# Cached attention and a Mish MLP with all gradients, one token: from a scheduled to a hand-ordered kernel

## The chip, the cores and the metric

The kernel runs on one core of a Trainium2 chip. The time is device microseconds of one execution; three executions of the kernel before took 449.38, 461.4 and 462.18 us, the median is 461.4 us. Lower is better. The profile is that of one execution.

## What is computed

One token `x` of width D = 640 goes through two branches that a gate mixes. Branch A has H = 32 heads of Dh = 128 over a cache of Sk = 4096 rows. All tensors are bf16.

```python
g = sigmoid((x * gate_w).sum(-1))
q = (x @ wq).reshape(32, 128)                    # per head
p = softmax(q @ K.T * Dh**-0.5)                  # 4096 scores of one query
a = (p @ V).reshape(4096) @ wo
h = x @ w1 + b1                                  # F = 1728
act = h * tanh(log1p(exp(-abs(h))) + max(h, 0))  # Mish
out = g * a + (1 - g) * (act @ w2)
```

The kernel returns `out` and, for a given `grad_out`, the gradients of x, K, V, wq, wo, w1, b1, w2 and gate_w. For the branch A and one head these are, with `do` the gradient of the head's output: `dp = V do`, `ds = p * (dp - sum(p * dp))`, `dq = K^T ds`, `dK = ds x q`, `dV = p x do` (outer products), `dwq = x x dq`, `dwo = o x da`. K and V are 33.5 MB each and are read once; dK and dV are as large and written once, so that the kernel moves some 168 MB.

## The kernel before

A cache row sits on partition p and block j: 128 partitions times J = 32 blocks of 128 elements. One head is one pass of `head` (L236), four heads are a group (G = 4), which shares one slice of wq and wo.

The instructions are written in a natural order and put into each engine's queue by the framework's scheduler, which goes by dependencies and priorities; the softmax statistics stand under `high_priority` (HP). It may place the next head's transposes among this head's work where buffers allow.

In a head, TensorE transposes K block by block (L254, 32 bf16 transposes of 128x128, eight to a PSUM tile; ScalarE copies a tile at a time, L255). Each transposed block is then the weight of a product with one moving column, q (L263, 32 of them), so that the scores lie as [128, 32]. The maximum over all rows needs the partitions: VectorE reduces along j (L268), ScalarE lays the result on a diagonal (L270, `dgm`), TensorE spreads it with a matrix of ones (L271, `MM`), VectorE takes the maximum (L273, `negM`). ScalarE's exponential (L275) gives e and its row sums, a product with ones their total (L276, `Zb`), then 1/Z (L278, `rz`) and p in duplicate (L280, `p_bf`). V goes the same way (L254, L255), its products with `do` (L285) give dp. L289 forms p*dp and its sums, L291 their total (`Db`), L293 and L295 ds. DQ (L298) and OP (L303) use K and V as they were loaded, 32 one-column products each, whose 32 result columns VectorE adds (L301, L306). Two small products per head take o to `a` (L311) and dq to dx (L315), the latter with transposed wq. The outer products (L324) are two halves of 2048 elements for dV and two for dK on VectorE, stored whole from GpSimd's queue (L332, L335). ScalarE forms the head's dwo (L336).

Per group, `prep_group` (L200) forms q on all partitions (L203, five 512-wide products), transposes wo (L193) to form `do` (L217), and transposes wq for dx; `finish_group` (L338) spreads dq by a diagonal from GpSimd (L340) and a product (L343), and VectorE forms dwq from PSUM (L347).

All K, V, wq and wo loads are on SyncE's queue, three heads ahead (four buffers for K and for V); a group's weights are asked for in the second head of the group before. The MLP's forward half runs after head 8 (L351), its gradients in six chunks, every third head from head 10 (L398), with the outer products for dw1 and dw2 on GpSimd (L419, L431); w1 is read once for the forward half and again in chunks (L353, L404).

## Time and profile before

| what | value |
|---|---|
| median of three executions | 461.4 us (449.38 to 462.18) |
| span of the profiled execution, first to last instruction | 459.0 us |
| time of the profiled execution as a whole | its span is what is recorded of it |
| mean granted clock of TensorE | 0.750 |
| TensorE, VectorE, ScalarE, GpSimd busy | 382.5, 264.4, 248.5, 96.3 us |
| DMA | 167.81 MB, mean 366 GB/s |
| L254, all transposes of K and V | 2048, 210.2 us |
| L324, all outer products | 128, 159.1 us |

A row of the groups reads: line, engine, operation, output and inputs, count, then busy time, mean ns of one, and how long the engine sat idle before it, and for whom. PEld is TensorE's weight load, which runs beside the matmul before it; a mean duration of a matmul holds its latency, so that neighbours overlap, and the *pitch*, the distance from one start to the next, is what a burst costs. Some pitches and durations that the timeline shows:

| operation | time |
|---|---|
| bf16 transpose, 128 columns, clock 1.0 / 0.5 | pitch 55 / 107 ns |
| one-column product, bf16 | pitch 25 / 27 ns |
| 512-wide product | pitch 216 / 427 ns |
| fp32 weight load (L271), clock 1.0 / 0.5 | 108 / 217 ns |
| fp32 product 128 wide (L271), two passes | 327 ns |
| outer half (L324) | 1.25 us, pitch 1.14 |
| copy 128x512 (L255) | 583 ns, pitch 482 |
| 128x512 product from PSUM (L347) | 682 ns, pitch 598 |
| 96x640 sum (L415) | 870 ns, pitch 800 |
| dwo of a head (L336) | 828 ns, pitch 730 |
| table load of ScalarE, five of them | 1283 ns each |
| DMA packet of 8192 / 5120 / 1280 / 1024 B | 309 / 199 / 55 / 46 ns |

### The profile page before, as it was taken

The page shows a single profiled execution, that of the slowest core. Times are in us where ns is not written, and L with a number is a line of the kernel's source. Part 1 is how long each engine was busy: PE and PEld are TensorE (multiplying, and loading weights), DVE is VectorE, ACT ScalarE, POOL GpSimd, SP SyncE. Part 2 cuts the span into 40 slices and gives each one's busy share as a digit, 9 for nine tenths or more (in the row PEclk, how much of TensorE's full clock was granted, in tenths as well). Part 3 has the DMA queues.
Part 4 walks back from the last instruction along what each step waited for, and adds up shares of the span by engine and source line. Part 5 has one row for each costly group of instructions (what it writes and reads, how often), then busy time and mean ns, then how long its engine had stood idle before and what let it go on. Part 6 is the DMA issues. An engine that isn't in the chain of part 4 may idle for free.

```text
span 459.0 us, 16426 instructions
## 1 busy us (share of the span) xinstructions
PE 382.5 (83%) x7301; PEld 350.4 (76%) x7320; DVE 264.4 (58%) x693; ACT 248.5 (54%) x571; POOL 96.3 (21%) x109
## 2 busy tenths in 40 slices
PE   0898989959899899969989599899999959999930
PEld 0688969838798788858888588887999858989820
DVE  0355735633627357737477488565656736665782
ACT  1575766626717777534665356656756536654510
POOL 0001010100100443551317141041000501014020
PEclk9998988859956699665987579587955879655555
DMA  8979999999999999999999999999999999973593
GB/s 248 427 308 349 411 425 417 413 416 334 418 422 360 369 360 363 420 354 406 420 418 370 386 386 375 420 406 394 413 424 419 364 348 347 416 284 127 206 365 118
DMA packets 45560, 167.81 MB, mean 366 GB/s; under 512 B 3122, under 2 KB 27506, under 8 KB 29106
## 3 DMA queue, kind: packets, MB, share of 16 engines
q1 hardware_dynamic: 25161, 84.24, 48.5%
q0 software_dynamic: 10368, 71.54, 38.0%
q10 hardware_dynamic: 9961, 10.99, 7.0%
q8 instruction: 57, 0.93, 0.8%
q14 instruction: 13, 0.11, 0.1%
HBM read 84.73 MB, written 82.03 MB: 363 GB/s over the span
## 4 chain that ended last, share of the span: by engine, by line
PE 61%; DMA 22%; ACT 7%; DVE 6%; issue 3%; ACTq 0%; SPq 0%; DVEq 0%
PE tr L254 25%; DMA wq_g<-in_A_wq_dram 10%; PE wtr_ps L193 6%; DMA wo_g<-in_A_wo_dram 5%; PE ss L298 5%; PE ss L285 5%; PE ss L303 5%; PE ss L263 4%; DMA w2c<-in_B_w_dram 3%; PE qbc_ps L203 3%; PE dobc_ps L217 2%; DMA xg_bc<-in_gate_w_dram 2%; PE ss L271 2%; ACT VT L255 2%; ACT KT L255 2%
## 5 line engine op out<-in xcount | busy, mean ns | idle before, releaser
L254 PE MATMUL tr<-ident_bf,Kn 128*128 128x128 bf16 x1024 | 105.1, 250 | 3.8 <-issue 1.2
L254 PE MATMUL tr<-ident_bf,Vn 128*128 128x128 bf16 x1024 | 105.1, 256 | 3.9 <-ACT VT L255 3.2
L255 ACT COPY VT<-tr 128x512 f32<-128x512 f32 x128 | 74.0, 583 | 53.0 <-PE tr L254 51.4
L255 ACT COPY KT<-tr 128x512 f32<-128x512 f32 x128 | 73.5, 585 | 42.3 <-PE tr L254 41.4
L254 PEld LDWEIGHTS <-Kn 128*128 128x128 bf16 x1024 | 81.0, 116 | 7.9 <-issue 6.1
L254 PEld LDWEIGHTS <-Vn 128*128 128x128 bf16 x1024 | 80.6, 117 | 5.9 <-issue 4.2
L324 DVE TENSOR_TENSOR dV_sb<-p_bf,qd_sb 128x2048 bf16<-128x2048 bf16 x64 | 80.6, 1264 | 4.8 <-ACT p_bf L280 4.8
L324 DVE TENSOR_TENSOR dK_sb<-ds_bf,qd_sb 128x2048 bf16<-128x2048 bf16 x64 | 78.5, 1229 | 0.3
L332 POOL DMA_DIRECT2D out_dram<-dV_sb x32 | 17.8, 555 | 164.4 <-DVE negD L293 80.4
L335 POOL DMA_DIRECT2D out_dram<-dK_sb x32 | 17.4, 544 | 144.5 <-DVE dK_sb L324 76.8
L263 PE MATMUL ss<-qTs_g,KT 128*128 128x1 bf16 x1024 | 40.9, 165 | 3.9 <-issue 2.1
L263 PEld LDWEIGHTS <-KT 128*128 128x128 bf16 x1024 | 37.3, 101 | 5.2 <-issue 3.0
L285 PEld LDWEIGHTS <-VT 128*128 128x128 bf16 x1024 | 34.1, 100 | 4.5 <-issue 2.3
L285 PE MATMUL ss<-doTs_g,VT 128*128 128x1 bf16 x1024 | 34.5, 164 | 2.1 <-ACT VT L255 1.1
L298 PEld LDWEIGHTS <-Kn 128*128 128x128 bf16 x1024 | 30.7, 99 | 6.6 <-issue 5.7
L298 PE MATMUL ss<-ds_bf,Kn 128*128 128x1 bf16 x1024 | 31.5, 164 | 4.6 <-issue 2.6
L303 PEld LDWEIGHTS <-Vn 128*128 128x128 bf16 x1024 | 31.2, 100 | 1.8 <-issue 1.4
L303 PE MATMUL ss<-e_bf,Vn 128*128 128x1 bf16 x1024 | 31.8, 164 | 0.7 <-issue 0.4
L347 DVE TENSOR_TENSOR dwq_g<-dqbc_ps,cols_f 128x512 bf16<-128x512 f32 x40 | 26.1, 682 | 5.6 <-DMA out_dram<-dwq_g 4.2
L203 PE MATMUL qbc_ps<-wq_g,cols_bf 128*128 128x512 bf16 x33 | 14.0, 535 | 16.2 <-DMA wq_g<-in_A_wq_dram 8.3
L273 DVE TENSOR_REDUCE negM<-ss 128x1 f32<-128x128 f32 x32 | 9.3, 290 | 30.9 <-PE ss L271 30.9
L278 DVE RECIPROCAL rz<-ss 128x1 f32<-128x1 f32 x32 | 5.4, 169 | 30.8 <-PE ss L276 30.8
(331 smaller groups left out, 522.2 us busy)
## 6 DMA issues: line engine op xcount, KB each, us to landing
Kn<-in_A_k_cache_dram SPq DMA_DIRECT2D x32, 1024.0 KB, 9.5
Vn<-in_A_v_cache_dram SPq DMA_DIRECT2D x32, 1024.0 KB, 16.1
out_dram<-dV_sb POOLq DMA_DIRECT2D x32, 1024.0 KB, 9.7
out_dram<-dK_sb POOLq DMA_DIRECT2D x32, 1024.0 KB, 10.2
wq_g<-in_A_wq_dram SPq DMA_DIRECT2D x8, 640.0 KB
wo_g<-in_A_wo_dram SPq DMA_DIRECT2D x8, 640.0 KB, 16.5
out_dram<-dwo_g ACTq DMA_DIRECT2D x8, 640.0 KB, 11.6
out_dram<-dwq_g ACTq DMA_DIRECT2D x8, 640.0 KB, 3.3
```

Source lines behind the costliest of these rows:

```text
L193: nc.tensor.transpose(tp[:, t, :], blocks[i + t], ident_bf[:])
L203: nc.tensor.matmul(qbc_ps[:], lhsT=x_col_bf[:, rc:rc + 1].to_broadcast([P, P]), rhs=wq_g[:, rc, :], start=(rc == 0), stop=(rc == RC - 1))
L254: nc.tensor.transpose(tp[:, t, :], src[:, c * TB + t, :], ident_bf[:])
L255: nc.scalar.copy(f32view(dst[:, c * TB:(c + 1) * TB, :].rearrange("p a b -> p (a b)")), f32view(tp[:].rearrange("p a b -> p (a b)")),)
L263: nc.tensor.matmul(S[:, j:j + 1], lhsT=KT[:, j, :], rhs=gp["qTs_g"][:, hh:hh + 1], start=True, stop=True)
L285: nc.tensor.matmul(DP[:, j:j + 1], lhsT=VT[:, j, :], rhs=gp["doTs_g"][:, hh:hh + 1], start=True, stop=True)
L298: nc.tensor.matmul(DQ[:, j:j + 1], lhsT=Kn[:, j, :], rhs=ds_bf[:, j, 0:1], start=True, stop=True)
L303: nc.tensor.matmul(OP[:, j:j + 1], lhsT=Vn[:, j, :], rhs=e_t[:, j:j + 1], start=True, stop=True)
L324: nc.vector.tensor_tensor(dst[:, a:b, :].rearrange("p j (a b) -> p j a b", b=2), colsrc[:, a:b, :].unsqueeze(2).to_broadcast([P, n, Dh // ...
L332: nc.gpsimd.dma_start(dVv[h], dV_sb[:])
L335: nc.gpsimd.dma_start(dKv[h], dK_sb[:])
L347: nc.vector.tensor_tensor(dwq_g[:, rc, :], dqbc_ps[:], x_col_f[:, rc:rc + 1].to_broadcast([P, GD]), ALU.mult)
```

## The change

The function is written anew. `manual_schedule()` puts the instructions into each engine's queue in the order of the program. The parts:

- **Pair transposes.** K and V are viewed as fp32, two bf16 values to an element, and transposed in 16 fp32 transposes of 128x128 instead of 32 of bf16, through three PSUM buffers. The copies stay 128x512 of fp32, four to an operand. Even and odd elements then lie interleaved, so a product takes every second bf16 as its weights, two products accumulate a pair of blocks, and q and do are laid out in zero-padded pairs of columns (`qd`, `dd`).
- **64-wide products.** All products of a head have a moving operand of 64 columns, one or two columns repeated. DQ and OP accumulate over the 32 blocks in PSUM, so that one column is the result and no reduction follows.
- **wq and wo untransposed.** Rows of wo are regrouped so that do comes from four 640-wide sums on VectorE per group (`prep_do_stt`), dx from five 512-wide sums (`fin_dx`); dwq comes from a copied row in SBUF (`fin_dwq`). `a` is formed once per group (`fin_orow`).
- **Order.** `period(h)` is a head without its K part. The next head's K transposes and products are in it: a quarter of the transposes before `Db`, a quarter after OP, the rest with all products after DQ. Group and MLP work is in three slots: A after `negM`, B after DQ, C after dK.
- **Queues.** wq and wo are loaded from ScalarE's queue, dwq and dwo stored from GpSimd's; V has three buffers, K four; V(h+3) and K(h+4) are asked for at the end of head h.
- **MLP.** w1 is read once and whole, w2 in two halves; all outer products and sums are on VectorE, spread over heads 5 to 30, with the 1728-wide dx sums in heads 27 and 29. Mish is formed from exponentials alone, without the logarithm, tanh and sigmoid.

```diff
+wq_v = A_wq.rearrange("(p rc) c -> p rc c", p=P)
...
+wo_v = A_wo.rearrange("(g p i) n -> g p i n", p=P, i=G)
...
+ctx.enter_context(tc.manual_schedule())
...
+def load_wq(g, eng):
+    wqs[g] = wts.tile([P, RC, GD], BF16, name="wq_g", tag="wq_g")
+    eng.dma_start(wqs[g][:], wq_v[:, :, g * GD:(g + 1) * GD])
+def load_wo(g, eng):
+    wos[g] = wts.tile([P, G, D], BF16, name="wo_g", tag="wo_g")
+    eng.dma_start(wos[g][:], wo_v[g])
...
-            nc.tensor.transpose(tp[:, t, :], blocks[i + t], ident_bf[:])
...
-        nc.tensor.transpose(qT_ps[:, hh, 0:1], qd_sb[0:1, 0, hh * Dh:(hh + 1) * Dh], ident_bf[0:1, 0:1])
...
-        nc.tensor.matmul(dobc_ps[:], lhsT=da_col_bf[:, c:c + 1].to_broadcast([P, P]),
-                         rhs=woT_g[:, c, :], start=(c == 0), stop=(c == RC - 1))
...
+    for rc in range(RC):
+        nc.tensor.matmul(ps[:], lhsT=x_col[:, rc:rc + 1].to_broadcast([P, P]), rhs=wqs[g][:, rc, :],
+                         start=(rc == 0), stop=(rc == RC - 1))
+    row = wts.tile([P, GD + Dh], BF16, name="qrow", tag="qrow")
+    nc.scalar.copy(row[:, 0:GD], ps[:])
+    nc.scalar.copy(row[0:1, GD:GD + Dh], ps[0:1, 0:Dh])
...
+    for hh in range(G):
+        nc.tensor.transpose(cp[:, hh:hh + 1], rf[0:1, hh * 64:hh * 64 + P], ident_f[0:1, 0:1])
...
+    nc.scalar.mul(dst[0:64, :, :, 0], cpb[0:64], mul)
...
+    nc.vector.scalar_tensor_tensor(junk[:], in0=wos[g][:, i, :], scalar=1.0, in1=da_bc[:], op0=ALU.mult,
+                                   op1=ALU.mult, accum_out=dof[g][:, i:i + 1])
...
+    for i in range(G):
+        nc.tensor.matmul(ps[:, i * P:(i + 1) * P], lhsT=dob[:, i:i + 1].to_broadcast([P, P]), rhs=ident[:],
+                         start=True, stop=True)
...
+    nc.scalar.copy(row[:, 0:GD].rearrange("m (p i) -> m p i", i=G), pv)
+    nc.scalar.copy(row[0:1, GD:GD + Dh].rearrange("m (p i) -> m p i", i=G), pv[0:1, 0:Dh // G, :])
...
+    for hh in range(G):
+        nc.tensor.matmul(ps[:, hh * P:(hh + 1) * P], lhsT=obfs[g][:, hh:hh + 1].to_broadcast([P, P]), rhs=ident[:],
+                         start=True, stop=True)
+    orow = small.tile([1, GD], BF16, name="orow", tag="orow")
+    nc.scalar.copy(orow[:], ps[0:1, :])
...
+    for i in range(G):
+        nc.tensor.transpose(op[:, i, 0:1], ov[:, i, :], ident[0:1, 0:1])
...
+    nc.vector.tensor_copy(opb[:], op[:, :, 0])
+    opf = small.tile([P, G], F32, name="opf", tag="opf")
+    nc.vector.tensor_copy(opf[:], opb[:])
...
+    for c in range(RC):
+        for i in range(G):
+            nc.tensor.matmul(ap[:, c:c + 1], lhsT=wos[g][:, i, c * P:(c + 1) * P], rhs=opb[:, i:i + 1],
+                             start=(i == 0), stop=(i == G - 1))
+    nc.vector.tensor_tensor(aT_acc[:], aT_acc[:], ap[:], ALU.add)
...
+    nc.scalar.activation(dwos[g][:, i, :], da_bc[:], ACT.Copy, scale=osc[g][:, i:i + 1])
...
+    for hh in range(G):
+        nc.tensor.matmul(ps[:, hh * P:(hh + 1) * P], lhsT=dqbfs[g][:, hh:hh + 1].to_broadcast([P, P]), rhs=ident[:],
+                         start=True, stop=True)
+    row = wts1.tile([P, GD], BF16, name="dqrow", tag="dqrow")
+    nc.scalar.copy(row[:], ps[:])
...
+    nc.vector.tensor_scalar(dwqs[g][:, rc, :], dqrow[g][:], x_col_f[:, rc:rc + 1], None, ALU.mult)
...
+    nc.vector.scalar_tensor_tensor(junk[:, 0:GD], in0=wqs[g][:, rc, :], scalar=1.0, in1=dqrow[g][:], op0=ALU.mult,
+                                   op1=ALU.mult, accum_out=dx_parts[:, rc, g:g + 1])
...
-                nc.tensor.transpose(tp[:, t, :], src[:, c * TB + t, :], ident_bf[:])
-            nc.scalar.copy(
-                f32view(dst[:, c * TB:(c + 1) * TB, :].rearrange("p a b -> p (a b)")),
-                f32view(tp[:].rearrange("p a b -> p (a b)")),
-            )
...
-        nc.tensor.matmul(S[:, j:j + 1], lhsT=KT[:, j, :], rhs=gp["qTs_g"][:, hh:hh + 1], start=True, stop=True)
...
-        nc.tensor.matmul(DQ[:, j:j + 1], lhsT=Kn[:, j, :], rhs=ds_bf[:, j, 0:1], start=True, stop=True)
...
-            nc.vector.reduce_sum(st["dq_bf_g"][:, hh:hh + 1], DQ, axis=AX.X)
...
-    nc.vector.tensor_scalar(ojunk[:], OP, rz[:], None, ALU.mult, ALU.add, accum_out=o32[:])
...
-        nc.tensor.matmul(aTp[:, c:c + 1], lhsT=gp["wo_g"][:, hh, c * P:(c + 1) * P], rhs=o_bf[:, 0:1],
-                         start=True, stop=True)
...
-        nc.tensor.matmul(dxTp[:, rc:rc + 1], lhsT=gp["wqT_g"][:, hh, rc, :], rhs=st["dq_bf_g"][:, hh:hh + 1],
-                         start=True, stop=True)
...
-    nc.gpsimd.tensor_tensor(diag[:], ident_bf[:].unsqueeze(1).to_broadcast([P, G, P]),
-                            st["dq_bf_g"][:].unsqueeze(2).to_broadcast([P, G, P]), ALU.mult)
...
-        nc.vector.tensor_tensor(dwq_g[:, rc, :], dqbc_ps[:], x_col_f[:, rc:rc + 1].to_broadcast([P, GD]), ALU.mult)
...
+def transposes(src, dst, c):
+    tp = tr_ps.tile([P, 4, P], F32, name="tr", tag="tr")
+    sf = f32v(src[:].rearrange("p j d -> p (j d)"))
+    for t in range(4):
+        jp = 4 * c + t
+        nc.tensor.transpose(tp[:, t, :], sf[:, jp * P:(jp + 1) * P], ident_f[:])
+    nc.scalar.copy(dst[:, 4 * c:4 * c + 4, :], tp[:])
+def products(T_, cols, dst, c):
+    tb = T_[:].bitcast(BF16).rearrange("r a (p b) -> r a p b", b=2)
+    for t in range(4):
+        jp = 4 * c + t
+        for par in range(2):
+            nc.tensor.matmul(dst[:, 2 * jp:2 * jp + W], lhsT=tb[:, jp, :, par],
+                             rhs=cols[:, par, :].unsqueeze(1).to_broadcast([P, W // 2, 2]),
+                             start=(par == 0), stop=(par == 1))
...
+    nc.vector.reduce_max(m32[:], S, axis=AX.X)
+    dgm = small.tile([P, P], F32, name="dgm", tag="dgm", bufs=2)
+    nc.scalar.activation(dgm[:], ident_s[:], ACT.Copy, scale=m32[:])
+    transposes(Vn, VT, 0)
+    transposes(Vn, VT, 1)
+    nc.tensor.matmul(MM, lhsT=ones_f[:], rhs=dgm[:], start=True, stop=True)
+    negM = small1("negM")
+    nc.vector.tensor_reduce(negM[:], MM, axis=AX.X, op=ALU.max, negate=True)
+    run(h, "A")
+    e_bf = small.tile([P, J], BF16, name="e_bf", tag="e_bf")
+    rowsum = small1("rowsum")
+    nc.scalar.activation(e_bf[:], S, ACT.Exp, bias=negM[:], scale=scale, accum_out=rowsum[:])
+    transposes(Vn, VT, 2)
+    transposes(Vn, VT, 3)
+    ddc = dds[g % 2][:, hh]
+    products(VT, ddc, sv[:, 0:128], 0)
+    products(VT, ddc, sv[:, 0:128], 1)
+    nc.tensor.matmul(Zb, lhsT=ones_f[:], rhs=rowsum[:], start=True, stop=True)
+    rz = small1("rz")
+    nc.vector.reciprocal(rz[:], Zb)
+    p_bf = small.tile([P, J, 2], BF16, name="p_bf", tag="p_bf")
+    nc.scalar.activation(p_bf[:], e_bf[:].unsqueeze(2).to_broadcast([P, J, 2]), ACT.Copy, scale=rz[:])
+    products(VT, ddc, sv[:, 0:128], 2)
+    products(VT, ddc, sv[:, 0:128], 3)
+    dV = outs.tile([P, J, Dh], BF16, name="dV", tag="dV")
+    dorow = dorows[g][:, hh * Dh:(hh + 1) * Dh]
+    outer(dV, p_bf, dorow, 0, HJ)
...
+    nc.vector.scalar_tensor_tensor(pj[:], in0=DP, scalar=1.0, in1=e_bf[:], op0=ALU.mult, op1=ALU.mult,
+                                   accum_out=part[:])
+    outer(dV, p_bf, dorow, HJ, J)
+    nc.gpsimd.dma_start(dVv[h], dV[:])
+    if h + 1 < H:
+        k_transposes(h + 1, 0)
+    nc.tensor.matmul(Db, lhsT=ones_f[:], rhs=part[:], start=True, stop=True)
+    for j in range(J):
+        nc.tensor.matmul(OP, lhsT=Vn[:, j, :], rhs=e_bf[:, j:j + 1].to_broadcast([P, W]),
+                         start=(j == 0), stop=(j == J - 1))
+    if h + 1 < H:
+        k_transposes(h + 1, 1)
+    negD = small1("negD")
+    nc.vector.tensor_scalar(negD[:], Db, rz[:], -1.0, ALU.mult, ALU.mult)
+    ds_bf = small.tile([P, J, 2], BF16, name="ds_bf", tag="ds_bf")
+    nc.vector.scalar_tensor_tensor(ds_bf[:], in0=DP.unsqueeze(2).to_broadcast([P, J, 2]), scalar=negD[:],
+                                   in1=p_bf[:], op0=ALU.add, op1=ALU.mult)
+    for j in range(J):
+        nc.tensor.matmul(DQ, lhsT=Kn[:, j, :], rhs=ds_bf[:, j, 0:1].to_broadcast([P, W]),
+                         start=(j == 0), stop=(j == J - 1))
+    run(h, "B")
+    if h + 1 < H:
+        for c in range(4):
+            if c < 2:
+                k_transposes(h + 1, c + 2)
+            k_products(h + 1, c)
+    dK = outs.tile([P, J, Dh], BF16, name="dK", tag="dK")
+    qrow = qrows[g][:, hh * Dh:(hh + 1) * Dh]
+    outer(dK, ds_bf, qrow, 0, HJ)
+    nc.vector.tensor_copy(dqbfs[g][:, hh:hh + 1], DQ[:, 0:1])
+    nc.vector.tensor_scalar(obfs[g][:, hh:hh + 1], OP[:, 0:1], rz[:], None, ALU.mult)
+    outer(dK, ds_bf, qrow, HJ, J)
+    nc.gpsimd.dma_start(dKv[h], dK[:])
+    run(h, "C")
+for g in range(NG - 1):
+    h0 = G * g
+    if g >= 1:
+        at(h0 + 1, "A", load_wo, g + 1, nc.scalar)
+        at(h0 + 1, "C", load_wq, g + 1, nc.scalar)
+    for i in range(2):
+        at(h0 + 2, "C", prep_do_stt, g + 1, i)
+        at(h0 + 3, "A", prep_do_stt, g + 1, 2 + i)
+    at(h0 + 3, "A", prep_q, g + 1)
+    at(h0 + 3, "B", prep_qcols, g + 1)
+    at(h0 + 3, "C", prep_do_row, g + 1)
+    at(h0 + 3, "C", prep_docols, g + 1)
+    f0 = h0 + G
+    at(f0, "A", fin_orow, g)
+    at(f0, "B", fin_dqrow, g)
+    for i in range(G):
+        at(f0, "C", fin_dwo, g, i)
+    at(f0, "C", store_dwo, g, nc.gpsimd)
+    for rc in range(RC):
+        at(f0, "C", fin_dwq, g, rc)
+    at(f0, "C", store_dwq, g, nc.gpsimd)
+    for rc in range(2):
+        at(f0, "C", fin_dx, g, rc)
+    for rc in range(2, RC):
+        at(f0 + 1, "A", fin_dx, g, rc)
...
-    nc.sync.dma_start(w1_sb[:], w1_v)
...
-    nc.sync.dma_start(w2c[:], w2_v[:, f0:f1, :])
-    w1c = mlp.tile([P, RC, FW], BF16, name="w1c", tag="w1c")
-    nc.sync.dma_start(w1c[:], w1_v[:, :, c * FW:(c + 1) * FW])
...
-        nc.vector.scalar_tensor_tensor(junk[:], in0=w2c[:, i, :], scalar=dm[:, f0 + i:f0 + i + 1], in1=dbp[:],
-                                       op0=ALU.mult, op1=ALU.mult, accum_out=ms["dh32"][:, f0 + i:f0 + i + 1])
...
-    nc.gpsimd.tensor_tensor(dw2c[:], act_bf[:, f0:f1].unsqueeze(2).to_broadcast([FP, FCC, D]),
-                            db_bc_bf[0:FP, :].unsqueeze(1).to_broadcast([FP, FCC, D]), ALU.mult)
-    nc.gpsimd.dma_start(dw2_v[:, f0:f1, :], dw2c[:])
...
-    nc.gpsimd.tensor_tensor(dw1c[:], dh_bc[:].unsqueeze(1).to_broadcast([P, RC, FW]),
-                            x_col_f.unsqueeze(2).to_broadcast([P, RC, FW]), ALU.mult)
-    nc.gpsimd.dma_start(dw1_v[:, :, c * FW:(c + 1) * FW], dw1c[:])
...
-        nc.vector.scalar_tensor_tensor(junk2[:], in0=w1c[:, rc, :], scalar=1.0,
-                                       in1=dhbc_ps[:], op0=ALU.mult, op1=ALU.mult,
...
+    nc.sync.dma_start(ml["w1"][:], w1_v)
...
+        nc.tensor.matmul(ps[0:n, 0:1], lhsT=lw, rhs=x_col[:, rc:rc + 1], start=(rc == 0), stop=(rc == RC - 1))
...
+    nc.vector.scalar_tensor_tensor(junk[0:n, :], in0=w, scalar=ml["dm"][0:n, i:i + 1], in1=db_bc[0:n, :],
+                                   op0=ALU.mult, op1=ALU.mult, accum_out=ml["dhf"][0:n, i:i + 1])
...
+            nc.tensor.matmul(ps[:, c:c + 1], lhsT=w[:, c * P:(c + 1) * P], rhs=ml["act"][0:n, i:i + 1],
...
+    nc.vector.tensor_scalar(w, db_bc[0:n, :], ml["actf"][0:n, i:i + 1], None, ALU.mult)
...
+    nc.vector.scalar_tensor_tensor(w, in0=w, scalar=1.0, in1=ml["dhrow"][:], op0=ALU.mult, op1=ALU.mult,
+                                   accum_out=dx_parts[:, rc, NG:NG + 1])
...
+    nc.vector.tensor_scalar(ml["w1"][:, rc, :], ml["dhrow"][:], x_col_f[:, rc:rc + 1], None, ALU.mult)
...
+M0 = 5
+for i in range(NF):
+    at(M0 + i // 5, "B", mlp_h, i)
+at(M0 + 4, "C", mlp_act)
+mp = [h for h in range(M0 + 5, 31) if h % 4 in (1, 2, 3)]
...
+    for i in (2 * k, 2 * k + 1):
+        if i < FH:
+            at(mp[k], "C", mlp_dh, i)
...
+for rc in range(RC):
+    at(mp[13] if rc < 3 else mp[14], "C", mlp_dx, rc)
+    at(mp[13] if rc < 3 else mp[14], "C", mlp_dw1, rc)
...
+prep_q(0)
+prep_qcols(0)
+for i in range(G):
+    prep_do_stt(0, i)
+prep_do_row(0)
+prep_docols(0)
+for c in range(4):
+    k_transposes(0, c)
+for c in range(4):
+    k_products(0, c)
+load_wq(1, nc.scalar)
+load_wo(1, nc.scalar)
+for h in range(H):
+    period(h)
+    if h + 3 < H:
+        load_v(h + 3)
+    if h + 4 < H:
+        load_k(h + 4)
+    if h == 1:
+        mlp_load_w1()
+    if h == 4:
+        mlp_load_w2(0)
...
+g = NG - 1
+mlp_store_dw1(nc.sync)
+mlp_store_dw2(1, nc.sync)
+fin_orow(g)
+for i in range(G):
+    fin_dwo(g, i)
+store_dwo(g, nc.sync)
+fin_dqrow(g)
+for rc in range(RC):
+    fin_dwq(g, rc)
+store_dwq(g, nc.sync)
+for rc in range(RC):
+    fin_dx(g, rc)
```

## The prediction

> **What bounds the kernel now.** I read three views in this order: the page's busy table with its chain, the groups, and the windows with their granted clock.
>
> ```profile
> PE 382.5 (83%) x7301; PEld 350.4 (76%) x7320; DVE 264.4 (58%) x693; ACT 248.5 (54%) x571; POOL 96.3 (21%) x109
> ...
> PEclk9998988859956699665987579587955879655555
> ...
> DMA packets 45560, 167.81 MB, mean 366 GB/s; under 512 B 3122, under 2 KB 27506, under 8 KB 29106
> ...
> PE 61%; DMA 22%; ACT 7%; DVE 6%; issue 3%; ACTq 0%; SPq 0%; DVEq 0%
> ```
>
> TensorE is busy for 83% of the span and holds 61% of the chain; the transfers hold 22%, mostly in the wait for the next group's wq and wo. Two limits lie close together. The queues' packets fill 94.4% of 16 engines' span (the shares of section 3 added), about 433 us, and TensorE fills 383 us. The PEclk row is the third thing to see: 9s at the start, only 5s in the last five slices.
>
> ```profile
> L254 PE MATMUL tr<-ident_bf,Kn 128*128 128x128 bf16 x1024 | 105.1, 250 | 3.8 <-issue 1.2
> L254 PE MATMUL tr<-ident_bf,Vn 128*128 128x128 bf16 x1024 | 105.1, 256 | 3.9 <-ACT VT L255 3.2
> L255 ACT COPY VT<-tr 128x512 f32<-128x512 f32 x128 | 74.0, 583 | 53.0 <-PE tr L254 51.4
> ...
> L324 DVE TENSOR_TENSOR dV_sb<-p_bf,qd_sb 128x2048 bf16<-128x2048 bf16 x64 | 80.6, 1264 | 4.8 <-ACT p_bf L280 4.8
> ...
> L347 DVE TENSOR_TENSOR dwq_g<-dqbc_ps,cols_f 128x512 bf16<-128x512 f32 x40 | 26.1, 682 | 5.6 <-DMA out_dram<-dwq_g 4.2
> ```
>
> 2048 transposes take 210 us of TensorE; this is what the change halves in number. The outer products on VectorE stay as they are.
>
> The windows show the granted clock (columns: window, its length, then busy us of PE, PEld, DVE, ACT and POOL, then clock, DMA share, GB/s):
>
> ```profile
> 58.00:61.40 3.40, 3.35 (x65) 2.61 (x63) 2.90 (x7) 2.77 (x6) 0.53 (x1) 1.00 1.01 426
> ...
> 93.10:96.50 3.40, 0.00 (x0) 0.00 (x0) 1.12 (x1) 0.00 (x0) 0.53 (x1) 0.52 1.04 421
> 391.70:404.00 12.30, 12.30 (x261) 12.22 (x261) 7.00 (x19) 7.51 (x17) 1.06 (x2) 0.58 1.01 416
> ```
>
> The clock is 1.0 or 0.5 in stretches of 3.41 us. In the third window TensorE is busy without a gap and yet has 0.58, so busy time does not earn the clock. Counting the moving columns of the matmul records in each stretch does separate the cases: full-clock stretches with at most 2626 columns were followed by half clock, those with at least 2852 stayed, so about 835 columns per us are needed. One-column products (32 take 0.94 us) stream almost nothing. A head of before streams 64 transposes x 128 = 8192 columns, 128 of its products, 256 of the maximum matmul and some 2690 of group work, 11,270 in 14.3 us (459/32), or 790 per us: just under the line, which is the mean clock of 0.75.
>
> The Trainium skill, "TensorE: Matmul & The Clock Gate", Part 1, has the clock fall after an idle window of about 3.4 us; by it the third window above would have kept full speed and so would nearly all of the new kernel, which by it comes to the 445 worked out below, by the columns to 474. The measured 0.58 decides against that.
>
> **The chain of a plain head.** The new kernel runs in written order, so I laid one head out by before's rows, with 0.04 us from engine to engine (read from the timeline). reduce_max 0.19, dgm 0.40, then ACT holds the copies of two V blocks ahead of the exponential (0.58 and 0.48), exponential 0.38, two more copies 1.06, p 0.35: 3.6 us with the steps between. MM, negM, Zb and rz (0.33, 0.29, 0.24, 0.17) lie beside the copies. Then VectorE does half of dV 1.25, pj 0.19, the other half 1.14, negD 0.16, ds 0.28: 6.6. From there TensorE needs DQ (32 at 25 to 27 ns, 0.85), eight transposes of the next K and 32 products 0.85, against dK on VectorE (1.25, 1.14 and two small ones), which ends at 9.2.
>
> **The pair transpose** is not in the trace. The bounds: a bf16 128-column transpose has a pitch of 55 ns at full clock, the lower end; an fp32 weight load (L271) takes 108 ns, its pair of passes 327 ns. I take 108 ns, since a pair transpose has to load 128x128 of fp32 as L271 does, and keep 55 and 213 (two such loads) for the range. Eight then cost 0.86 on the chain, and the head ends at **9.4 us**; with 55 ns 8.8. Sixteen per operand instead of 32 thus cost the same 1.7 us by 108 ns: the halving is worth nothing on TensorE unless the pitch is the lower one.
>
> The same page, "Weight-path perf modes", says the fast weight load is off for FP32; this speaks against the pair form. By its rule the load is the slow one, as L271's row has it; the sum with it is the one above, without it 10 us lower over the kernel.
>
> The **64-wide products** cost 26.7 ns at full clock against 25 for one column (the weight load bounds both), 53 against 27 at half clock. They bring columns: 32 transposes x 128, 128 products x 64 and 256 make 12,540 per head. If a plain head runs 9.4 us that is 1330 per us, well over 835. The weights of the K and V products are read with a step of two elements; no row has that. At best nothing is lost, at worst they load like fp32 (108 ns): 64 x 83 = 5.3 us per head. I take nothing, since every bf16 row of 128 columns shows the 25 ns pitch, and keep a loss for the range. The column reductions L301 and L306 become small copies, under 0.2 us a head gained.
>
> **Group work.** It leaves 40 transposes, five 512-wide dobc matmuls and L194's copies per group on TensorE and ACT, and comes back on VectorE in the chain. Per group, by the rows: the o row before the exponential makes VectorE and TensorE wait for each other (four matmuls, a copy, four transposes, two copies, 20 products: 1.9 us); dwq (five SBUF-only scalar products; between L278's 169 ns for one column and the 444 ns of a 128x288 sum, L436; taken 0.25) and two dx sums (0.6, L347's pitch) 2.5, and the dq row 0.3; three more dx sums 1.8; four 640-wide do sums (0.8 each, L415's pitch) and q's row 2.9. That is 9.4 per group, 66 for seven.
>
> **The MLP** was on POOL, PE and DVE beside the heads; now it is in the chain: h 14 x 0.5, the activation as some 24 dependent small operations 4.5, dh 14 x 0.8, dw2 14 x 0.3, b 1.8, the dh row 3.0, five 1728-wide dx sums 1.9 each (1728 elements at the rate of L415's 640 in 0.67 above its start) and five dw1 0.55: 43 us. The four table loads of 1.28 us saved count for nothing more than 5.
>
> **The sum at full clock.** Head 0's maximum came at 24.6 us; now wo lands at about 9, then four sums 3.3, row and columns 1.5, K's transposes and products 3.4: 17. 31 heads x 9.4 = 291. Side work 66 + 43 - 5 = 104. After the last maximum: the head 9.4, o row 1.9, dq row 0.9, dwq and dx 4.3, small operations 2.5, transposes and copies 1.2, the store 2: 22. Together 434.
>
> Transfers: K, V, dK and dV in 8192-byte packets of 309 ns are 2048 packets over 16 engines, 9.9 us a head, 316 us; the weights and the rest at their rows' medians some 82: 398, and 420 with the 5% by which before's queues exceed this. w1 is loaded once, not twice. The floor is below 434, but loads are issued at a head's end behind others, and w1's 2.2 MB stand ahead of K. The three plain heads in a row near the start outrun the queue. I add 11 of 0 to 16: **445**.
>
> **The clock.** In a long head VectorE's last slot lies between dK and the next maximum; V's first eight transposes run ahead into three PSUM buffers and then TensorE waits for the maximum: 1.1 us of dK, 2.5 of side work and 0.6, over 4 us without columns in a finishing head, more beside dx of the MLP (13 us of it at head 27). The following stretch is then at half clock. There a head needs 32 x 0.216 + 128 x 0.053 + 1.5 = 15.2 us of TensorE, so a stretch of 3.41 us yields 3.41 x 9.4/15.7 = 2.05 and loses 1.36. Some 17 heads last over 12 us; with 1.3 such stretches after each, 22 x 1.36 = 30. The sum is **474 us** against the span of 459.0, which lies 2.4 below the median of 461.4; I leave this within the range.
>
> **Rivals.** *The clock stays up* (chance 0.27, the one on the other side): the 64-wide columns fill enough of each stretch, or a pair transpose counts more than 128 columns. For it: 12,540 columns a head. Against it: VectorE's slots leave over 4 us empty. It gives 434 to 452. It decides from five half-clock stretches downwards (445 + 5 x 1.36 = 452).
>
> *The pair transpose or the stepped weights are dear* (0.20): at 213 ns the 32 transposes add 3.4 us a head, about two thirds of it on the chain, 70 us over 31, and starve the clock; 500 to 550. For it: L271's rows; against it: one operand passes once where L271 passes twice.
>
> *The rewrite only moves the limit to the transfers* (0.11): before's queues are full for 94% of its span and 2 MB per head are stored and loaded as before; with some wait for late loads, 452 to 472.
>
> **How the numbers follow.** Forecast, 455 to 495, has 0.42. Measured times can tell about 2% from no change: below 452.2 is faster, above 470.6 slower. Faster 0.27 from the first rival and the edges. The forecast gives 0.15 within and 0.27 above; the transfers 0.06 and 0.05; dear transposes 0.20 above: 0.21 and 0.52. The range reaches from 437, which leaves some 0.08 of the first rival out, to 520, which leaves half of the dear case.
>
> **What would show it.** Plain heads (the distance of two row maxima, heads 1 to 3) of 9 to 10 us; the pitch of the transposes at 0.108 us in a burst at full clock; TensorE idle before the maximum matmul for over 2 us in finishing heads with a granted clock of 0.5 right after; a mean clock of 0.75 to 0.85; the DMA share below 0.95; one table load. Wrong it is if the mean clock is above 0.95, if a transpose takes over 0.15 us, or if VectorE waits mostly for transfers.

## The result, and the profile after

The new kernel is **slower**: median 533.46 us of four executions (529.37 to 538.52) against 456.87 us for the kernel before; the ratio is 1.180, with a 95% interval of 1.167 to 1.192. Ratios, here and below, are formed from undisturbed executions alone (here 529.37 to 535.33 against 449.38 and 452.33), so they differ a little from those of the medians. The profiled execution took 529.37 us, with a span of 527.6 us. The forecast was 474 us with a range of 437 to 520: the direction was right, the size was not, and the time lies outside the range.

These are the lines of the new kernel's page that answer to those shown of before: busy times, clock, packets, the chain, and the groups.

```profile
PE 373.2 (71%) x5864; PEld 335.3 (64%) x5871; DVE 303.1 (57%) x770; ACT 227.1 (43%) x523; POOL 45.8 (9%) x85
...
PEclk9999989888788889896978969889598797788795
...
DMA packets 29499, 164.93 MB, mean 313 GB/s; under 512 B 3226, under 2 KB 9118, under 8 KB 12543
...
PE 40%; DMA 24%; DVE 20%; ACT 12%; issue 3%; ACTq 1%; DVEq 0%
...
L464 PE MATMUL tr<-ident_f,Kn 128*128 128x128 f32 x512 | 88.7, 302 | 0.0
L489 DVE TENSOR_TENSOR dV<-p_bf,dorow 128x2048 bf16<-128x2048 bf16 x64 | 78.3, 1223 | 15.2 <-ACT p_bf L544 15.2
...
L465 ACT COPY VT<-tr 128x512 f32<-128x512 f32 x128 | 69.2, 582 | 15.9 <-PE tr L464 15.6
...
L216 PE MATMUL grp<-wq_g,x_col 128*128 128x512 bf16 x33 | 15.3, 571 | 34.8 <-DMA wq_g<-in_A_wq_dram 33.6
```

No engine is full: TensorE fell from 83% to 71% of a longer span, and the transfers run at 313 GB/s in place of 366. The chain has changed from 61% TensorE to a row of engines that wait for each other. The clock got better, not worse: its mean is 0.864 against 0.750. The last line is the new one: TensorE stood idle for 34.8 us ahead of q's products, 33.6 of them because wq had not landed.

The distance from one head's row maximum (L523) to the next gives the heads one by one. This is worked out from the start times in the trace, four heads to a line, in us:

```
heads      new kernel                 wq on SyncE's queue (below)
 0 to  3   10.0  10.0  10.6  11.6     10.1  10.0  10.6  11.6
 4 to  7   16.4  16.8  14.7  20.0     16.3  16.6  14.8  14.8
 8 to 11   17.8  15.3  13.9  14.6     17.0  15.8  14.1  11.9
12 to 15   15.3  12.9  11.5  25.8     15.3  12.0  11.5  14.4
16 to 19   16.4  11.2  10.6  23.0     16.4  11.2  10.6  11.6
20 to 23   16.7  11.2  12.5  24.6     15.7  12.0  12.5  15.4
24 to 27   16.2  13.5  14.6  24.9     15.3  13.1  14.6  25.6
28 to 30   15.8  17.5  11.6           15.8  19.0  11.6
```

The plain heads 0 and 1 take 10.0 us. The first head of a group, which finishes the group before, takes 15 to 18. The fourth heads 7, 15, 19 and 23 take 20 to 26, and there lies most of what the forecast did not have. The timeline shows it in head 7 (columns: start, duration, engine and line, and in brackets the idle time before and who ended it):

```profile
115.75 0.18 DVE L523 TENSOR_REDUCE m<-sk 128x1 f32<-128x32 f32 x1
115.97 0.40 ACT L525 ACTIVATE dgm<-ident_s,m 128x128 f32<-128x128 f32 x1 [1.51 <-DVE m L523]
...
116.42 0.49 PE L528 MATMUL mm<-dgm,ones_f 128*128 128x128 f32 x2 [0.58 <-ACT dgm L525]
116.95 0.29 DVE L530 TENSOR_REDUCE negM<-mm 128x1 f32<-128x128 f32 x1 [1.01 <-PE mm L528]
...
120.64 1.72 PE L216 MATMUL grp<-wq_g,x_col 128*128 128x512 bf16 x4 [3.73 <-DMA wq_g<-in_A_wq_dram]
```

`prep_q` stands in slot A, behind `negM` and ahead of V's last eight transposes. TensorE works in order, so the wait for the next group's wq holds this head's transposes of V. On ScalarE the copy of q's row (`qrow`, L219) stands ahead of the exponential, so it holds this head's softmax too (waits of the whole run: total, times, longest):

```profile
ACT qrow L219 <- PE grp L216: 49.4, 8, 12.2
...
PE grp L216 <- DMA wq_g<-in_A_wq_dram: 33.6, 6, 10.3
```

The load was issued at 99.8 us and its last packet ended 20.1 us later. In the chain that ended last, the same load and its like are the longest pieces by far (columns: start, duration, what):

```profile
99.75 20.84 DMA wq_g<-in_A_wq_dram
121.08 1.27 PE grp L216 x3
...
224.35 23.69 DMA wq_g<-in_A_wq_dram
248.89 1.48 PE grp L216 x3
...
289.52 21.94 DMA wq_g<-in_A_wq_dram
312.31 1.48 PE grp L216 x3
...
351.04 24.94 DMA wq_g<-in_A_wq_dram
376.83 1.49 PE grp L216 x3
```

A chain puts the whole transfer down, from its issue; what it cost is less, since the engines worked on for most of that time. Run 1 below measures it.

How a load can take so long shows in the packets between its issue and its end. A wq load is 640 packets of 1024 bytes (46 ns each, 1.8 us on 16 engines). Counted from the trace, with the packets of 4 KB and more that ran in the same time on the queue of the stores (q0) and on that of the K and V loads (q1):

```
kernel, queue of wq              issued at   last packet    q0 big   q1 big   16 engines busy
new, ScalarE's                      99.8        20.1 us       607      399       1.02
new, ScalarE's                     224.4        23.2 us       577      487       0.95
new, ScalarE's                     351.0        24.5 us       675      512       0.97
wq on SyncE's, line with K and V   152.1        15.4 us       631      118       1.02
wq on SyncE's                      209.0        15.7 us       666       98       1.02
wq a head earlier, ScalarE's       212.7        11.9 us       447      113       1.03
```

The packets add up to the time: 640 x 46 ns + 1006 x 309 ns, over 16 engines, is 21.3 us for the first row, against 20.1 measured. Where the engines are full such a sum must come out, in whatever order the packets ran. That the queues take turns shows within a load: in the third row's, from 356 to 371 us, when all three had work, 414 small packets ran beside 367 and 354 big ones, and the small ones took 8% of the engines' time. In the first row the turns are not all: nine tenths of the packets were through after 11.0 us, and the last tenth took nine us more; no run here shows why. The Trainium skill, "DMA: Bandwidth & Descriptors", section "Queues, rings and completion order", says that an engine goes round the queues with work packet by packet; the counts of the third row agree with it. An estimate by it and the packets' times: a queue of small packets beside two of big ones gets a fourteenth of the engines' time here (46 of 46 + 309 + 309).

### The profile page after: what moved, and what is told of

The parts are those of the page before. It is cut to its first block, busy times and chain, and to the rows that moved or that the text cites. A ratio compares the mean times of both kernels' runs of the same rounds, so it can differ in the third digit from the quotient of the medians.

```text
span 527.6 us, 13596 instructions
## 1 busy us (share of the span) xinstructions
PE 373.2 (71%) x5864; PEld 335.3 (64%) x5871; DVE 303.1 (57%) x770; ACT 227.1 (43%) x523; POOL 45.8 (9%) x85
## 2 busy tenths in 40 slices
DMA packets 29499, 164.93 MB, mean 313 GB/s; under 512 B 3226, under 2 KB 9118, under 8 KB 12543
## 4 chain that ended last, share of the span: by engine, by line
PE 40%; DMA 24%; DVE 20%; ACT 12%; issue 3%; ACTq 1%; DVEq 0%
DMA wq_g<-in_A_wq_dram 22%; PE tr L464 13%; DVE dV L489 6%; PE sk L560 5%; PE sk L570 5%; ACT dwo_g L290 4%; DVE junk L314 3%; PE sv L472 3%; PE grp L216 2%; DMA wo_g<-in_A_wo_dram 2%; DVE dK L489 2%; PE sk L472 2%; PE mm L558 2%; ACT p_bf L544 2%; PE mm L528 2%
## 5 line engine op out<-in xcount | busy, mean ns | idle before, releaser
L464 PE MATMUL tr<-ident_f,Kn 128*128 128x128 f32 x512 | 88.7, 302 | 0.0
L489 DVE TENSOR_TENSOR dV<-p_bf,dorow 128x2048 bf16<-128x2048 bf16 x64 | 78.3, 1223 | 15.2 <-ACT p_bf L544 15.2
L464 PE MATMUL tr<-ident_f,Vn 128*128 128x128 f32 x512 | 79.1, 305 | 0.0
L489 DVE TENSOR_TENSOR dK<-ds_bf,qrow 128x2048 bf16<-128x2048 bf16 x64 | 78.1, 1220 | 0.9
L465 ACT COPY VT<-tr 128x512 f32<-128x512 f32 x128 | 69.2, 582 | 15.9 <-PE tr L464 15.6
L464 PEld LDWEIGHTS tr<-ident_f,Vn 128*128 128x128 f32 x512 | 65.7, 157 | 3.0 <-issue 2.6
L464 PEld LDWEIGHTS tr<-ident_f,Kn 128*128 128x128 f32 x512 | 60.5, 154 | 0.1
L472 PEld LDWEIGHTS <-VT 128*128 128x128 bf16 x1024 | 53.1, 116 | 2.2 <-ACT VT L465 0.3
L472 PE MATMUL sv<-dd,VT 128*128 128x64 bf16 x1024 | 54.2, 214 | 0.1
L472 PE MATMUL sk<-qd,KT 128*128 128x64 bf16 x1024 | 49.5, 198 | 5.2 <-ACT KT L465 5.2
L472 PEld LDWEIGHTS <-KT 128*128 128x128 bf16 x1024 | 44.4, 101 | 10.1 <-ACT KT L465 8.7
L216 PE MATMUL grp<-wq_g,x_col 128*128 128x512 bf16 x33 | 15.3, 571 | 34.8 <-DMA wq_g<-in_A_wq_dram 33.6
L560 PEld LDWEIGHTS <-Vn 128*128 128x128 bf16 x1024 | 37.7, 102 | 0.0
L570 PEld LDWEIGHTS <-Kn 128*128 128x128 bf16 x1024 | 37.1, 99 | 0.8 <-issue 0.3
## 6 DMA issues: line engine op xcount, KB each, us to landing
Kn<-in_A_k_cache_dram SPq DMA_DIRECT2D x32, 1024.0 KB, 11.9
out_dram<-dV POOLq DMA_DIRECT2D x32, 1024.0 KB, 11.1
```

Source lines behind the costliest of these rows:

```text
L216: nc.tensor.matmul(ps[:], lhsT=x_col[:, rc:rc + 1].to_broadcast([P, P]), rhs=wqs[g][:, rc, :], start=(rc == 0), stop=(rc == RC - 1))
L464: nc.tensor.transpose(tp[:, t, :], sf[:, jp * P:(jp + 1) * P], ident_f[:])
L465: nc.scalar.copy(dst[:, 4 * c:4 * c + 4, :], tp[:])
L472: nc.tensor.matmul(dst[:, 2 * jp:2 * jp + W], lhsT=tb[:, jp, :, par], rhs=cols[:, par, :].unsqueeze(1).to_broadcast([P, W // 2, 2]), start ...
L489: nc.vector.tensor_tensor(dst[:, a:b, :].rearrange("p j (a b) -> p j a b", b=2), col[:, a:b, :].unsqueeze(2).to_broadcast([P, n, Dh // 2, 2]),
L560: nc.tensor.matmul(OP, lhsT=Vn[:, j, :], rhs=e_bf[:, j:j + 1].to_broadcast([P, W]), start=(j == 0), stop=(j == J - 1))
```

## The experiments

Each was timed together with the kernel before. "The new kernel" without more is the one above.

**1. wq on SyncE's queue.**

```diff
-            at(h0 + 1, "C", load_wq, g + 1, nc.scalar)
+            at(h0 + 1, "C", load_wq, g + 1, nc.sync)
```

> The new kernel with one word changed: from group 2 on wq is loaded from SyncE's queue, in line with K and V, and not from ScalarE's. Theory A (late wq): the new kernel's seven wq loads land 20 to 24 us after their issue because their 1024-byte packets take turns with the 8192-byte packets of two other queues, and q's products stand ahead of V's transposes in TensorE's order; the heads 7, 15, 19, 23 and 27, which last 20 to 26 us in place of 11 to 15, then lose some 50 us. It expects a landing under 15 us, TensorE's wait for wq under 10 us in all (38 us now) and 475 to 495 us. Theory B (the loss lies in the head's own chain, and the wait for wq only takes the place of other waits, for K, V or the stores): the wait moves to K and V and the time stays over 515.

Measured: 487.44 us (486.47 to 490.1), ratio 1.069 (1.058 to 1.080). The loads landed after 15 to 21 us, less improved than expected, but that was enough. In its waits, TensorE's for wq is 1.4 us in place of 33.6, and ScalarE's for q's row 13.3 in place of 49.4:

```profile
ACT qrow L219 <- PE grp L216: 13.3, 8, 5.0
...
PE grp L216 <- DMA wq_g<-in_A_wq_dram: 1.4, 2, 0.8
```

The medians lie 46 us apart, the two profiled executions 39.3. The right half of the table of heads shows where these come from: heads 7, 15, 19 and 23 fall to 12 to 15 us, 37 us together, head 11 by 2.7, and the others move little. The 31 distances add up to 437.4 us against 477.5: some **40 us** were the late wq. Theory A holds, theory B falls.

**2. wq loaded once**, the bound of what that wait can cost.

```diff
-            at(h0 + 1, "C", load_wq, g + 1, nc.scalar)
+            wqs[g + 1] = wqs[0]
...
-    load_wq(1, nc.scalar)
+    wqs[1] = wqs[0]
```

> The new kernel without the wq loads after the first: all groups use group 0's wq (so q, dq and what follows from them are those of other weights; 4.6 MB less are read). This is the bound of what the wait for wq can cost. Theory A expects 460 to 480 us and no head over 18 us but those with the 1728-wide sums; theory B over 505.

Measured: 490.30 and 492.93 us. With no wq to wait for after the first, the time is no lower than that of run 1. Nothing of the wait is left to gain there, and the 460 to 480 of theory A were too hopeful: some 30 us above the kernel before have another cause.

**3. wq a head earlier, still on ScalarE's queue.**

```diff
-            at(h0 + 1, "C", load_wq, g + 1, nc.scalar)
+            at(h0, "C", load_wq, g + 1, nc.scalar)
...
-        for rc in range(2):
-            at(f0, "C", fin_dx, g, rc)
-        for rc in range(2, RC):
-            at(f0 + 1, "A", fin_dx, g, rc)
+        for rc in range(RC):
+            at(f0, "C", fin_dx, g, rc)
```

> The new kernel with wq still on ScalarE's queue but asked for a head earlier: all five dx sums of the group before stand in slot C of the group's first head, and the load of the next group's wq follows them there, not in the second head. If the turns with the big packets are the reason for the long landing, it stays at 20 us or more, but one head of 11 to 16 us more lies ahead of its use, so TensorE's wait falls under 10 us and the time to 480 to 500. If the landing shortens to under 15 us as it did on SyncE's queue (where heads 7 to 27 took 12 to 15 us), the turns were not the reason. If the time stays over 515, the gain of the other run came from something else than the earlier arrival.

Measured: 507.56 and 508.27 us. No wait for wq is left in its list but 0.4 us for the first. But the landing was 11 to 12 us in five of the six loads, which by the words above speaks against the turns. The counts show another reading: at that point of a group q1 has only 90 to 113 big packets standing, not 269 to 512, and the row in the table above is 640 x 46 + 560 x 309 over 16 = 12.7 us, 11.9 measured. What stands in the other queues goes with the landing, as the turns have it; the fixed 20 us of the expectation were the mistake. The time is 20 us above run 1. Three more dx sums of 0.68 us stand in slot C of the finishing heads, which take 17.0 to 20.0 us there against 15.3 to 17.0, some 16 us over the seven.

**4. dwo elsewhere on ScalarE.**

```diff
+        run(h, "E")
...
-            at(f0, "C", fin_dwo, g, i)
-        at(f0, "C", store_dwo, g, nc.gpsimd)
+            at(f0 + i // 2, "E", fin_dwo, g, i)
+        at(f0 + 1, "C", store_dwo, g, nc.gpsimd)
```

> The new kernel with ScalarE's four dwo rows of a group moved from slot C of the group's following head, where they stand ahead of the next head's diagonal (dgm), to behind p of that head and of the one after it, two and two. Theory C (ScalarE's place: 2.3 us of dwo hold back dgm, seven times, and the clock falls in the gap): 10 to 20 us less, so 507 to 517. If VectorE's own work in slot C hides dwo, or the wq load swallows what is gained, within 4 us of the new kernel.

Measured: 532.48 us (525.07 to 541.44), ratio 1.158 (1.136 to 1.180), no difference that can be told from the new kernel: theory C's 10 to 20 us are not there. (Slot E is new here, behind p.) What dwo is worth where wq is in time was not tried alone.

**5. Products of two columns.**

```diff
-    W = 64
+    W = 2
```

> The new kernel with products 2 columns wide in place of 64 (K and V products one pair, DQ and OP one column twice). Theory D (the columns earn the clock, as the prediction has it): 128 x 62 columns a head go, some 4600 remain in 10 to 25 us, under the 835 per us that before's trace asked for; the mean clock falls from 0.86 towards 0.5 to 0.6 and the time rises by 50 us or more. If the fp32 transposes alone keep the clock (each counted as more than 128 columns, or by busy time), the mean clock stays over 0.8 and the time within 10 us.

Measured: 550.36 us (549.04 to 552.08), ratio 1.205 (1.191 to 1.220), mean clock 0.573. The columns do earn the clock, as the prediction had it; the loss is 17 us and not 50. The wait for wq was in the chain anyway, and longer heads (plain ones 12.8 to 13.2 us) leave it more time: TensorE's wait for wq falls from 33.6 to 7.8 us, and of the fourth heads only one still takes over 20 us before head 27. A window of this run shows why busy time is not the measure (columns as in the windows of before):

```profile
150.00:170.00 20.00, 17.13 (x212) 15.69 (x212) 9.71 (x27) 11.41 (x25) 2.53 (x4) 0.50 0.54 195
```

TensorE is busy for 17.1 of 20 us and gets half clock throughout. The transposes show what that costs, 415 ns each in place of 302:

```profile
L464 PE MATMUL tr<-ident_f,Kn 128*128 128x128 f32 x512 | 133.8, 415 | 0.0
```

**6. Without the MLP**, on top of run 1: its loads, sums, outer products and stores are left out.

```diff
-    M0 = 5
-    for i in range(NF):
-        at(M0 + i // 5, "B", mlp_h, i)
...
-        if h == 1:
-            mlp_load_w1()
-        if h == 4:
-            mlp_load_w2(0)
...
-    mlp_store_dw1(nc.sync)
-    mlp_store_dw2(1, nc.sync)
```

> The new kernel with wq on SyncE's queue (487 us) and without the MLP branch: no w1, b1, w2 loads, none of its sums, outer products or stores; dw1, dw2 and db1 are not written, out and dx lack its share. The prediction's sum has the MLP at 43 us of the chain: 440 to 450. If its work lies beside other work, 470 or more.

Measured: 428.55 and 430.31 us. This is the cleanest view of the prediction's sum, since neither the late wq nor the MLP is in it. The heads repeat group by group: 15.6 to 15.7, 11.2 or 12.0, 10.6, 11.6, together 49.1 to 49.9 us. The MLP costs 487.4 - 429.4 = 58 us in the chain (43 in the sum, hence the 440 to 450 expected), with the half clock that it brings: 109 us of the span are at half clock with it and 43 without.

**7. The maximum ahead of slot C**, on top of run 1.

```diff
         nc.gpsimd.dma_start(dKv[h], dK[:])
+        if h + 1 < H:
+            maximum(h + 1)
         run(h, "C")
```

> The new kernel with wq on SyncE's queue (487 us) and the next head's row maximum and diagonal ahead of slot C's work on VectorE and ScalarE. Theory E (TensorE waits for the maximum behind slot C): about 1 us of each filled slot C lies beside the diagonal and its product, some 20 heads, and 1.5 us of dwo in seven heads: 458 to 472. If the work only moves to the next wait, since negM stands behind it now, 480 to 490.

Here `maximum` stands for the row maximum and `dgm`. Measured: 491.25 us (490.48 to 493.47) against 487.44. Theory E falls. The maximum's rows of both kernels, run 1 first, say why (who ended the idle time of its engine, us, times):

```profile
  DVE m L523: 37.4, 18
  PE sk L472: 14.5, 9
```

```profile
  PE sk L472: 35.9, 29
  DVE m L508: 23.9, 31
```

In a plain head VectorE is done 0.85 us before TensorE has the next scores. In run 1 slot C's work filled that time; with the maximum in front VectorE waits for the scores in 29 heads, and slot C's work then stands ahead of `negM`. One wait took the place of the other.

**8. The pair transposes undone**, on top of run 1.

```diff
-        tp = tr_ps.tile([P, 4, P], F32, name="tr", tag="tr")
-        for t in range(4):
-            nc.tensor.transpose(tp[:, t, :], sf[:, jp * P:(jp + 1) * P], ident_f[:])
+        tp = tr_ps.tile([P, 8, P], BF16, name="tr", tag="tr")
+        for t in range(8):
+            nc.tensor.transpose(tp[:, t, :], src[:, 8 * c + t, :], ident[:])
...
-                nc.tensor.matmul(dst[:, 2 * jp:2 * jp + W], lhsT=tb[:, jp, :, par],
+            nc.tensor.matmul(dst[:, j:j + W], lhsT=tb[:, j, :], rhs=cols[:, 0, 0:1].to_broadcast([P, W]),
...
```

> The new kernel with wq on SyncE's queue (487 us) and the pair transposes undone: 32 bf16 transposes per operand in the same order, eight to a PSUM tile, then one 64-wide product per block instead of two per pair. A pair transpose has a pitch of 109 ns in the new kernel's trace, a bf16 one of 55 in that of before, so by the pitch 16 of the one cost what 32 of the other do: 480 to 494, with the same columns per head and the same mean clock of 0.88 to 0.90. If the halved number of instructions is worth something beside the pitch, 500 or more.

Measured: 486.40 us (484.81 to 487.85), ratio 1.070 (1.061 to 1.079), clock 0.905: the same as run 1. The median pitches are 55.5 ns here and 109 ns for a pair, at half clock 107 and 213. The pair form is worth nothing here, as the prediction had it.

**9. Filling TensorE's wait for the maximum**, on top of run 1.

```diff
+        if (h - 1, "C") in fill:
+            for i in range(10):
+                nc.tensor.matmul(mm[:, 256:512], lhsT=ident[:], rhs=da_bc[:, 0:256], start=True, stop=True)
         nc.tensor.matmul(MM, lhsT=ones_f[:], rhs=dgm[:], start=True, stop=True)
```

> The new kernel with wq on SyncE's queue (487 us, mean clock 0.89) and ten more products of 256 columns, whose result nobody reads, ahead of the maximum product in each head that follows a filled slot C. They take 1.07 us at full clock and 2.13 at half, in TensorE's wait for the maximum (1.5 to 4.6 us there). If the half clock after these waits costs what the prediction's sum has for it (about 1.4 us for each stretch, 30 in all), the clock rises over 0.95 and the time falls to 460 to 478. If those stretches are bound by VectorE and ScalarE, the clock rises and the time stays at 482 to 492; if the products delay the maximum, 495 or more.

Measured: 492.97 us (492.12 to 495.76), ratio 1.084 (1.077 to 1.092); the clock rose to 0.923, and half clock fell from 109 to 78 us of the span. Heads with the same work let the two effects be parted: head 12, at full clock in both, went from 15.3 to 16.1 us, so the filling costs 0.7 there; head 4 lost its 3.4 us of half clock and went from 16.3 to 16.4, so that stretch had cost about 0.6. The prediction had 1.36. In head 4 half clock hides in part, presumably since VectorE and ScalarE hold that head; head 21 lost one stretch too and fell from 12.0 to 11.2 in spite of the filling, so the price differs from head to head. The time lies between the expectation's second case and its third: the filling itself delays the maximum. What all half-clock stretches cost together was not measured.

**10. wo first**, on top of run 1: the first group's wo behind wq on SyncE's queue.

```diff
     load_wq(0, nc.sync)
+    load_wo(0, nc.sync)
     load_k(0)
...
-    load_wo(0, nc.scalar)
```

> The new kernel with wq on SyncE's queue (487 us) and the first group's wo asked for on SyncE's queue too, behind wq and ahead of K. In the new kernel wo lands at 14.5 us, where the prediction had 9, and the first row maximum comes at 25.7 (25.9 with wq on SyncE's queue). By the trace do's sums can start when the gate's row is there, at 9.0: the first maximum at about 20 and the time 5 to 6 us less, 481 to 483. If K, now later, holds the start, or the gained start is lost to later waits, 486 to 489.

Measured: 486.66 us (481.57 to 487.94). The first maximum came 4.3 us earlier, at 21.6, and the span is 2.7 shorter; over the heads 2 us were given back, and the medians cannot be told apart.

**11. The work spread over the gaps.** The whole schedule once more by what the runs had shown by then: wq on SyncE's queue, wo ahead of K at the start, no side work in front of the exponential, VectorE's side work in pieces, new slots M (ahead of the maximum product), Z (behind `rz`), E (behind p), F (ahead of `Db`) and G (behind o); each 1728-wide sum is cut in two. Its core:

```diff
-        at(h0 + 3, "A", prep_q, g + 1)
-        at(h0 + 3, "C", prep_do_row, g + 1)
-        at(f0, "A", fin_orow, g)
-            at(f0, "C", fin_dwo, g, i)
-            at(f0, "C", fin_dwq, g, rc)
+        at(h0 + 3, "M", prep_do_m, g + 1)
+        at(h0 + 3, "E", prep_do_e, g + 1)
+        at(h0 + 3, "F", prep_q, g + 1)
+        at(f0, "M", fin_orow_m, g)
+        at(f0, "E", fin_orow_e, g)
+        at(f0, "F", fin_orow_f, g)
+            at(f0 + 1 + i // 2, "F", fin_dwo, g, i)
+            at(f0 + 1, "Z", fin_dwq, g, rc)
+            at(f0 + 2, "Z", fin_dwq, g, rc)
...
+    hs = [(27, "A"), (27, "C"), (28, "A"), (28, "A"), (29, "C"), (29, "C"), (30, "A"), (30, "A"), (30, "C"), (30, "C")]
+    for n, (h, sl) in enumerate(hs):
+        at(h, sl, mlp_dx, n // 2, n % 2)
...
```

> The whole kernel once more by these findings: wq on SyncE's queue, wo asked for ahead of K at the start, the maximum ahead of slot C, dwo on ScalarE beside the outer products, q's and do's rows, the o row and the MLP's h products where TensorE waits for the total of p*dp, dx, dwq, do and the MLP's sums in pieces of under 1 us spread over the gaps behind the maximum, negM and rz, dw1 stored in two parts. If the side work of some 104 us in the prediction's sum is what remains above the transfers, it falls by some 60 us, and 11 us go at the start: 425 to 450, bound by the transfers (420). If heads stay as long (clock, or VectorE's share), 465 or more.

Measured: **427.37 us** (425.75 to 428.69), 33 us below the median of 460.58 of the kernel before, timed with it, and 23 below that kernel's fastest execution there (450.80).

```profile
PE 343.1 (80%) x5864; PEld 313.4 (73%) x5871; DVE 301.9 (71%) x776; ACT 223.4 (52%) x519; POOL 46.4 (11%) x87
...
PEclk9999999999999699999999888999989989899775
...
DMA packets 29594, 164.93 MB, mean 386 GB/s; under 512 B 3241, under 2 KB 9069, under 8 KB 12638
```

Nearly the same work per engine as in the new kernel (VectorE 302 us, ScalarE 223) stands in a span 100 us shorter. Most heads take 10 to 12 us, the finishing ones 11.0 to 11.1 up to head 20; the fourth of a group takes 13.1 to 14.5, and some others 13 to 20 (head 10 beside the activation, head 19 with its wait for w2, several of heads 24 to 30 with the MLP's last work). The mean clock is 0.936, and the transfers run at 386 GB/s: their packets, by section 3 of the page, fill 95.8% of 16 engines' span, against 79.7% in the new kernel. Which of the many changes gives how much was not tried one by one.

**12. One sum later.** In run 11 head 19 waited 5.6 us for w2; its sum was moved to head 24.

```diff
-    for i, (h, sl) in enumerate(((19, "A"), (19, "C"), (20, "A"), (22, "A"), (22, "C"), (23, "A"), (23, "C"))):
+    for i, (h, sl) in enumerate(((19, "C"), (20, "A"), (22, "A"), (22, "C"), (23, "A"), (23, "C"), (24, "A"))):
```

> The spread kernel (427 us) with one of its MLP sums moved from head 19, where it waited 5.6 us for w2, to head 24. The wait was on the chain of head 19 (20.0 us, other heads of its place 13.4): 3 to 6 us less, 421 to 425. If the transfers set the time, it stays at 427.

Measured: 431.57 us (427.48 to 433.42), ratio 0.948 (0.941 to 0.954). Head 19 went from 20.0 to 13.4 us, but head 23 from 13.7 to 22.1: the wait moved on, with transfers at 22% of the chain in place of 12%. The 421 to 425 expected did not come. It gives the interval by which the spread form beats the kernel before; between the two forms, timed apart and 1% from each other, it does not decide.

## Why the prediction was wrong

The prediction's terms beside what the runs show of each, in us; the sum of the measured column is the span of 527.6 within 1:

| term | predicted | measured | from |
|---|---|---|---|
| to the first maximum | 17 | 25.7 | new kernel's timeline |
| 31 plain heads | 291 | 310 | heads 0 and 1, 10.0 each |
| group work, with its half clock | 66 | 66 | run 6: 376 us of heads less 310 |
| MLP, with its half clock | 38 | 62 | spans of run 1 less run 6, 488.3 - 426.8 |
| half clock, of both | 30 | in the two rows above | not parted |
| late loads | 11 | 40 | heads of the new kernel less run 1 |
| after the last maximum | 22 | 24.5 | new kernel's timeline |

Of the 53 us between this sum and the span, late loads are 29, plain heads 19, the first maximum 9 and the end 2; group work, MLP and clock together came out 6 lower than forecast (134 and 128).

- **The step that failed is "I add 11 of 0 to 16"** for loads that come late. It measured 40. The section on transfers had the total of bytes and packets, and its 420 us were right (the new kernel's packets fill 79.7% of 527.6 us, 420), but it did not ask of each load when it is issued, beside what, and who stands behind its first reader. Its reason named K behind w1; in the new kernel no engine's list of waits has one for K or V, and TensorE's has 33.6 us for wq. wq was moved to a queue of its own, where small packets take turns with big ones, and its reader stands in the middle of a head on an engine that works in order. With wq in time (run 1) the time is 487, inside the range.
- **The first maximum** was 8.7 late. 5.6 of this is the same mistake: "now wo lands at about 9"; its first sum could start at 14.6, on ScalarE's queue beside K and V. The rest lies behind it: K's transposes and products took 5.4 and not 3.4, do's row and columns 2.2 and not 1.5.
- **The plain head** of 9.4 measured 10.0, the second largest miss. The pair transpose was right (0.108 predicted, 0.109 measured). The 64-wide product was not: 31 ns, not 26.7, at full clock, with 64 of them on the chain 0.3 us; another 0.3 us TensorE's weight load waits for the copy of K's last blocks.
- **Group work** of 9.4 a group measured 49.1 to 49.9 less four times 10.0, 9.1 to 9.9, half clock included.
- **The clock** was right in its rule and wrong in its size. The new kernel streams enough columns for a mean of 0.864 (0.75 to 0.85 forecast); there are 43 half-clock stretches rather than 22, 11 more than in run 1 with wq in time. The one stretch of a finishing head that run 9 can price cost some 0.6 us rather than 1.36. More stretches at less each may have met the 30 us by luck; their sum was not measured.
- **The signs named** came in part: transposes at 0.109 us, one table load, a DMA share well below 0.95 and half clock in the finishing heads; the wait for the maximum there is nearer 1.8 us than the 4 that were reckoned, and longest where the 1728-wide sums stand (4.6 us after head 27 and 6.1 after head 29, in run 1 and the new kernel alike). None of the three signs of being wrong appeared. The third looked at VectorE, whose waits for transfers are 8 us, all at the start; the 33.6 us for wq were TensorE's.
- **The rivals.** The first one's reason came true in part, since a pair transpose counts as 256 columns (below), but not its condition: it asked for five half-clock stretches at most, and there are 43. The dear transposes did not come: nothing at 213 ns but at half clock, and the stepped weights of L472 load in 25 ns in run 5, as fast as any. The transfers came near to being the limit only in run 11.
- **Slips of the sum**, of a few us each: it adds up to 475, not 474; four do sums at 0.8 are 3.2 by themselves, more than the 2.9 given with q's row; a head has 512 packets of 8192 bytes, not 2048 (the 9.9 us are those of 512); the half-clock head takes 15.2 in one place and 15.7 in the next; and 0.6 us a head from the lower transpose pitch would be 19 us over the kernel, not 10.
- **Beyond the prediction**, the change's order, not its parts, is what costs time: nearly the same instructions in run 11, with wq and the first wo on SyncE's queue, take 427 us.
